# A windowed attention with a gated output layer: the last output block in two column halves, two blocks gathered in the scores' banks, and another written-out order

## Chip, cores and metric

The kernel runs on one core of one Trainium2 chip. The metric is device time in microseconds (us) of one launch. A core has TensorE (PE in the profile, with its weight loads as PEld), VectorE (DVE), ScalarE (ACT), GpSimd (POOL) and SyncE (SP). Here SP issues nearly all DMA transfers; ACT issues three at the start.

## What is computed

```python
# q, k, v: (4, 8, 768, 64) float32; w_val, w_out: (512, 512) float64; conv_w: (5, 512) float64
scores = q @ k.T / 8                       # kept where key < 4 (sinks) or 0 <= row - key < 128
a = softmax(scores, over kept keys);  x = a @ v           # heads joined: (4, 768, 512)
gate = sigmoid(causal 5-tap convolution of x along the rows, per column, weights conv_w)
out = ((gate * (x @ w_val)) @ w_out)       # (4, 768, 512) float32
```

## The kernel before

**Tiling.** The 768 rows of each of 4 batches are cut into 3 parts of 256 rows; with two quads of heads that makes 24 steps `s` (batch, part, quad). Two steps make one block `m` of 256 rows and all 512 columns, so there are 12 blocks. Each block gives two output blocks of 128 rows, `i` = 0 and 1.

**Stages of a step.** `kq`, `vv` load queries, keys and values (three buffers each). `s0`, `s1` are the score matmuls of two head pairs (line 391, on parts of 64x32 of the TensorE array), masked and reduced to a maximum on DVE; `e0`, `e1` are the exponentials on ACT; `rec` and `norm` normalise (ACT, DVE, POOL); `tx` transposes the weights on TensorE (line 449, whole array), `px` and `py` copy them out of PSUM; `sk`, `ts` do the same for the four sink keys (line 454, whole array); `vl` multiplies with the values (line 504, parts of 64x64) and `si` adds the sinks (line 511, whole array). `xc`, `xh`, `hd`, `xl`, `c4`, `c0`, `c1`, `th` take the result out of PSUM, split it into a high and a low part for exact products, and form the gate.

**Stages of a block.** `v0` to `v3` are the products with `w_val` (line 566), `v0`, `v1` the halves of one 512-column bank and `v2`, `v3` of the next; `g0`, `g1` gate them (DVE), `h0`, `h1`, `l0`, `l1` split again (ACT, POOL). `o0` and `o1` are the two halves of the contraction with `w_out` for output block 0 (`outp`, line 606), `o2` and `o3` those for block 1, and `t0`, `t1` copy the result out of PSUM with factor 0.5 (`store`, line 610) and store it (line 613). The weights come as float64 and are taken apart on the chip in stages `wv?` and `wo?` (`wvl` loads, `wva` to `wvf` decode).

**PSUM.** Of eight banks of 512 columns, four form two pairs `pr` that `scores` and `probs_t` take in turn through `pair()`, two hold `xv`, and two, `homes`, serve `val`, `outp`, the sinks' transposes and the weights' decoding: each takes one off the list and gives it back.

**Order.** The string `ORDER` names every stage once. Inside `tc.manual_schedule()` it is walked from left to right, and every engine runs its own instructions in that order (SP's DMA issues too); semaphores set the rest. `fill.n` are n TensorE matmuls on zeros. `flag`, computed on DVE, decides between this path and a general one (`tc.If`, line 781): each engine loads it into a register (line 780) and branches. Those loads stand outside the written-out order; the scheduler places them.

Of the kernel before, what the change touches and what calls it, by code (L numbers as in the profile page):

```python
# [36 lines left out]
blanks wvl.0 load_conv kq.0 masks signs leads fill.5 wvl.1 conv_weights wvl.2 wva.0 wvb.0 s0.0 kq.1 wvd.0
wvc.0 s1.0 wve.0 fill.4 wva.1 wvb.1 e0.0 wva.2 e1.0 wvb.2 wvc.2 fill.7 wvd.1 wol.0 kq.2 s1.1 wvc.1 rec.0 wvl.3
s0.1 fill.10 s1.2 wvf.0 woa.0 e1.1 wve.1 e0.1 wob.0 norm.0 tx.0 px.0 e1.2 woc.0 rec.1 py.0 vv.0 fill.6 sv.0
sk.0 ts.0 wod.0 wva.3 norm.1 s0.2 e0.2 vl.0 kq.8 kq.3 s0.3 wvf.1 si.0 xc.0 woe.0 wvb.3 xh.0 tx.1 c4.0 rec.2  # L40
wof.0 wol.2 wol.1 wvc.3 fill.6 hd.0 wvd.2 wve.2 px.1 wvd.3 kq.4 wve.3 e0.3 c0.0 c1.0 woa.1 wob.1 wvf.2 norm.2
vv.3 py.1 vv.1 sv.1 xl.0 tx.2 py.2 sk.1 px.2 woc.1 ts.1 vl.1 s1.3 wvf.3 wod.1 si.1 xc.1 c4.1 sk.2 ts.2 s0.4
hd.1 xh.1 xl.1 c0.1 woe.1 e1.3 wol.3 rec.3 woa.3 c1.1 wob.3 e0.4 v0.0 v1.0 th.0 y0.0 norm.3 vv.2 g0.0 vl.2
woa.2 wob.2 h0.0 l0.0 th.1 s1.4 kq.6 kq.5 wof.1 woe.3 e1.4 v2.0 v3.0 y1.0 tx.3 py.3 si.2 xc.2 woe.2 hd.2 xh.2
g1.0 px.3 wof.2 wod.2 s0.6 c4.2 c0.2 h1.0 o0.0 l1.0 o2.0 e0.6 wof.3 s0.5 c1.2 rec.4 xl.2 s1.6 wod.3 o1.0 o3.0
t0.0 norm.4 sk.3 e0.5 ts.3 t1.0 vl.3 si.3 xh.3 xc.3 xl.3 s1.5 e1.6 tx.4 px.4 vv.5 sk.4 ts.4 hd.3 c4.3 c0.3
e1.5 rec.5 norm.5 v0.1 v1.1 y0.1 py.4 c1.3 th.2 v2.1 v3.1 g0.1 h0.1 kq.7 s0.7 vv.4 th.3 vl.4 y1.1 g1.1 vv.6
l0.1 s1.7 rec.6 sv.6 s1.8 h1.1 si.4 xh.4 l1.1 xc.4 hd.4 e0.7 o2.1 o3.1 c4.4 c0.4 xl.4 e1.8 kq.10 kq.9 c1.4
norm.6 tx.5 o0.1 t1.1 py.5 o1.1 px.5 sk.5 e1.7 tx.6 rec.7 px.6 ts.5 t0.1 py.6 vl.5 si.5 xc.5 hd.5 xh.5 s0.9
e0.9 sk.6 ts.6 s0.8 e0.8 c4.5 c0.5 c1.5 xl.5 vv.7 v0.2 rec.8 v1.2 norm.7 tx.7 py.7 px.7 th.4 g0.2 v2.2 s1.9  # L50
s1.10 norm.8 th.5 h0.2 e1.9 vl.6 si.6 sk.7 vv.8 v3.2 ts.7 xc.6 hd.6 xh.6 l0.2 g1.2 rec.9 o0.2 c4.6 h1.2 l1.2
o2.2 o3.2 sv.7 e1.10 c0.6 kq.11 tx.8 c1.6 py.8 vl.7 px.8 norm.9 s0.10 si.7 t1.2 sk.8 xl.6 xc.7 hd.7 xh.7 ts.8
kq.12 c4.7 tx.9 px.9 c0.7 c1.7 e0.10 rec.10 py.9 xl.7 th.6 o1.2 norm.10 v0.3 v1.3 vv.10 g0.3 h0.3 s0.12 s0.11
t0.2 vl.8 si.8 s1.11 e0.12 xc.8 hd.8 c4.8 sk.9 ts.9 l0.3 kq.13 th.7 vv.9 xh.8 e0.11 e1.11 c0.8 c1.8 v2.3 v3.3
o2.3 xl.8 g1.3 s1.12 s1.13 vl.9 si.9 h1.3 tx.10 l1.3 o3.3 e1.12 rec.12 rec.11 px.10 xc.9 hd.9 xh.9 py.10 c4.9
c0.9 t1.3 o0.3 o1.3 c1.9 th.9 t0.3 sk.10 ts.10 xl.9 vv.11 norm.11 s0.13 vl.10 si.10 xc.10 c4.10 hd.10 xh.10
norm.12 kq.15 tx.11 px.11 py.11 th.8 e0.13 v0.4 v1.4 v2.4 v3.4 c0.10 c1.10 g0.4 sk.11 ts.11 e1.13 g1.4 h0.4
l0.4 kq.14 tx.12 py.12 vl.11 px.12 s0.14 s1.14 rec.13 si.11 h1.4 sk.12 ts.12 o0.4 l1.4 o1.4 vv.12 o2.4 o3.4
sv.12 xc.11 c4.11 hd.11 xh.11 c0.11 vv.13 c1.11 e0.14 sv.13 kq.18 s0.18 norm.13 e1.14 rec.14 kq.16 s0.15 xl.10
t1.4 vl.12 si.12 th.11 xc.12 hd.12 xh.12 xl.11 c4.12 t0.4 xl.12 tx.13 norm.14 px.13 v2.5 v3.5 c0.12 g1.5 py.13  # L60
th.10 c1.12 e0.15 v0.5 v1.5 g0.5 sk.13 ts.13 h0.5 l0.5 vv.14 s1.15 e1.15 s1.18 rec.15 kq.19 vl.13 si.13 xc.13
hd.13 xh.13 o0.5 s0.16 h1.5 kq.17 tx.14 px.14 c4.13 c0.13 c1.13 l1.5 o2.5 o3.5 th.12 e0.16 o1.5 norm.15 t1.5
py.14 warm_up tx.15 py.15 t0.5 sk.14 ts.14 s1.16 vl.14 si.14 vv.17 e1.18 xc.14 hd.14 xh.14 sk.15 ts.15 xl.13
px.15 e1.16 c4.14 vv.15 v2.6 v0.6 v1.6 c0.14 c1.14 rec.16 g0.6 s0.17 xl.14 e0.18 h0.6 e0.17 s0.19 rec.18 vl.15
norm.16 v3.6 l0.6 th.13 si.15 vv.16 g1.6 s1.19 xc.15 th.14 c4.15 hd.15 xh.15 s1.17 sk.16 o0.6 ts.16 kq.20 h1.6
l1.6 xl.15 tx.16 o1.6 v0.7 v1.7 e0.19 px.16 c0.15 e1.17 rec.17 t0.6 kq.21 c1.15 s0.20 py.16 vl.16 si.16
norm.18 vv.21 sk.18 ts.18 vv.18 e1.19 xc.16 hd.16 g0.7 norm.17 rec.19 e0.20 tx.18 px.18 py.18 c4.16 c0.16
th.15 xh.16 v2.7 v3.7 xl.16 h0.7 g1.7 tx.17 h1.7 px.17 l1.7 c1.16 py.17 o2.6 o3.6 s1.20 s0.21 t1.6 vl.17 sk.17
ts.17 l0.7 o0.7 si.17 e1.20 xc.17 hd.17 xh.17 norm.19 tx.19 c4.17 vv.19 c0.17 sv.18 c1.17 xl.17 o1.7 kq.22
o2.7 o3.7 py.19 e0.21 rec.20 norm.20 px.19 t1.7 s1.21 scalars vl.18 t0.7 si.18 xc.18 hd.18 xh.18 c4.18 c0.18  # L70
sv.19 th.17 tx.20 px.20 e1.21 vv.22 rec.21 th.16 v2.8 v3.8 v0.8 v1.8 g1.8 h1.8 c1.18 g0.8 sk.19 ts.19 py.20
h0.8 s1.22 kq.23 s0.22 vl.19 si.19 xc.19 hd.19 xh.19 xl.18 l1.8 sk.20 l0.8 vv.20 o0.8 ts.20 c4.19 c0.19 c1.19
norm.21 e1.22 e0.22 rec.22 o1.8 o2.8 tx.21 py.21 px.21 t0.8 vl.20 xl.19 s1.23 s0.23 si.20 xc.20 norm.22 hd.20
xh.20 e1.23 th.18 v0.9 v1.9 g0.9 c4.20 c0.20 e0.23 rec.23 o3.8 t1.8 tx.22 v2.9 v3.9 h0.9 py.22 c1.20 sk.21
l0.9 norm.23 th.20 ts.21 th.19 vl.21 si.21 g1.9 px.22 xc.21 hd.21 xh.21 tx.23 px.23 o0.9 o2.9 c4.21 c0.21
c1.21 h1.9 l1.9 xl.20 o3.9 t1.9 o1.9 py.23 sk.22 ts.22 t0.9 vl.22 xl.21 si.22 xc.22 sk.23 v0.10 v1.10 xh.22
# [113 lines left out]
def banded(ctx, tc, wts, cw, zero, ident, warm_up, scalars, flag, qt, kt, vt, vsk, w_val, conv_w, w_out, out):  # L190
# [406 lines left out]
    def outp(m, i, h):  # L597
        wh, wl = wts["wo"]
        gh, gl = gs[m]
        if h == 0:  # L600
            vacc[m, 2 + i] = homes.pop(0)
        acc = vacc[m, 2 + i]
        ts = slice(i * P, (i + 1) * P)
        for kc in (0, 1) if h == 0 else (2, 3):
            for n, (a, x) in enumerate(((gh, wh), (gh, wl), (gl, wh))):
                nc.tensor.matmul(acc, a[:, kc, ts], x[:, kc], start=(kc + n == 0), stop=(kc + n == 5))  # L606

    def store(m, i):
        ob = p2.tile([P, DM], F32, name="osb", tag="osb", bufs=3)
        nc.scalar.activation(out=ob, in_=vacc[m, 2 + i], func=AF.Copy, scale=0.5)  # L610
# [2 lines left out]
        nc.sync.dma_start(out=out[m // NP, at:at + P, :], in_=ob)

# [232 lines left out]
```

## Time and profile before

| | |
|---|---|
| median of 3 runs (lowest, highest) | 271.04 us (270.05, 272.22) |
| profiled execution: its time, its span | 270.55 us, 268.7 us |
| TensorE busy | 258.3 us (96%), 3760 matmuls |
| DVE, ACT, POOL busy | 205.4, 189.1, 176.2 us |
| DMA | 36.93 MB, mean 137 GB/s |
| last output copy starts, ends | 261.75, 262.35 us |

The span is the time between the first and the last event that the profile holds; the execution lies 1.85 us above it. Rows of the chain of waits and of the timeline give the start in us from the span's start, the length in us, the engine, the output tile (or output and input) and the line; a count x n stands behind merged rows. Groups of instructions give busy time and the mean ns of one. Matmuls overlap in the records, so a TensorE row of the chain (start to next start) is the better measure of what a matmul costs than its own length.

### The profile page before, as it was taken

The numbers are of one execution on the slowest core, as the hardware profiler recorded it, in microseconds if no ns is written. First come the engines' busy times: TensorE is split into PE (matmuls) and PEld (weight loads), VectorE is DVE, ScalarE is ACT, GpSimd is POOL, SyncE is SP. The second block draws the span as 40 slices with busy tenths as digits, with TensorE's granted clock in tenths as the row PEclk, the third lists the DMA queues.
The fourth block names the chain that finished last, engine by engine and source line by source line (L and its number), as shares of the span: only waits on it lengthen the run. The fifth ranks groups of instructions, "written<-read, shape, count | busy, mean of one in ns | idle before, by whom it ended". The sixth has DMA issues, their size and how long they took to land.

```text
span 268.7 us, 9474 instructions
## 1 busy us (share of the span) xinstructions
PE 258.3 (96%) x3760; PEld 213.6 (79%) x3760; DVE 205.4 (76%) x561; ACT 189.1 (70%) x667; POOL 176.2 (66%) x233
## 2 busy tenths in 40 slices
PE   7899999999999999999999999999999999999990
...
DMA packets 27394, 36.93 MB, mean 137 GB/s; under 512 B 2256, under 2 KB 23760, under 8 KB 27344
## 3 DMA queue, kind: packets, MB, share of 16 engines
...
q14 instruction: 19, 0.16, 0.2%
...
## 4 chain that ended last, share of the span: by engine, by line
PE 83%; ACT 9%; POOL 2%; DMA 2%; issue 1%; DVE 0%; POOLq 0%; ACTq 0%
PE ac L606 25%; PE ac L566 25%; PE xv L504 11%; PE pr L391 10%; PE pr L449 7%; ACT w L416 4%; PE xv L511 3%; DMA raw<-in_w_val_dram 2%; PE ac L454 1%; POOL xl L534 1%; ACT wvh L151 1%; ACT wv_p L137 1%; ACT wv_p L156 1%; ACT wvl L183 1%; POOL wo_f L157 0%
## 5 line engine op out<-in xcount | busy, mean ns | idle before, releaser
L547 DVE SCALAR_TENSOR_TENSOR sg<-xv,cw,sg 128x256 f32<-128x256 f32 x192 | 77.8, 474 | 12.4 <-POOL sg L539 7.0
L431 POOL TENSOR_TENSOR wx<-w,sm 128x512 f32<-128x512 f32 x48 | 49.1, 1044 | 11.3 <-DVE sm L423 11.1
L416 ACT ACTIVATE w<-pr,ngm 128x132 f32<-128x132 f32 x136 | 48.5, 369 | 1.7
L595 POOL TENSOR_TENSOR gl<-sg,gh 128x512 fp32r<-128x512 f32 x24 | 31.0, 1295 | 28.1 <-ACT gh L591 28.0
L566 PE MATMUL ac<-xh,wvh 128*128 128x256 f32 x192 | 48.4, 286 | 0.0
L566 PE MATMUL ac<-xh,wvl 128*128 128x256 f32 x192 | 47.1, 279 | 0.0
L606 PE MATMUL ac<-woh,gh 128*128 128x512 f32 x96 | 39.2, 408 | 0.0
L539 POOL TENSOR_TENSOR sg<-xt,cw 128x512 f32<-128x512 f32 x24 | 25.0, 1043 | 20.6 <-ACT xt L518 20.6
L606 PE MATMUL ac<-wol,gh 128*128 128x512 f32 x96 | 38.0, 396 | 0.0
L606 PE MATMUL ac<-woh,gl 128*128 128x512 f32 x96 | 38.0, 395 | 0.0
L566 PEld LDWEIGHTS ac<-xh,wvh 128*128 128x128 f32 x192 | 36.1, 188 | 0.8 <-issue 0.5
L566 PEld LDWEIGHTS ac<-xh,wvl 128*128 128x128 f32 x192 | 36.2, 188 | 0.2
L391 PE MATMUL pr<-k,q 64*32 64x168 f32 x1536 | 35.3, 307 | 0.7 <-DMA q<-in_qt_dram 0.6
L504 PEld LDWEIGHTS xv<-wt,v 64*64 64x64 f32 x1024 | 30.4, 133 | 7.0 <-issue 4.5
L504 PE MATMUL xv<-wt,v 64*64 64x192 f32 (+2 forms) x1024 | 34.5, 278 | 0.2 <-PE ac L566 0.2
L534 POOL TENSOR_TENSOR xl<-xt,xh 128x512 fp32r<-128x512 f32 x24 | 30.8, 1289 | 3.2 <-ACT xh L526 2.8
L566 PE MATMUL ac<-xl,wvh 128*128 128x256 f32 x192 | 30.7, 280 | 0.4 <-POOL xl L534 0.4
L391 PEld LDWEIGHTS pr<-k,q 64*32 64x32 f32 x1536 | 23.8, 106 | 7.9 <-issue 2.6
L396 DVE COPY_PREDICATED pr<-low,pr 128x256 f32<-128x256 uint8 x48 | 20.3, 423 | 12.2 <-PE pr L391 12.2
L591 ACT ACTIVATE gh<-sg 128x512 fp32r<-128x512 f32 x24 | 15.0, 628 | 19.2 <-DVE sg L585 19.2
L416 ACT ACTIVATION_READ_ACCUMULATOR w<-pr,ngm 128x1 f32 x136 | 27.6, 203 | 0.0
L518 ACT ACTIVATE xt<-xv 128x512 f32<-128x512 f32 x24 | 14.4, 600 | 17.3 <-PE xv L511 17.2
...
## 6 DMA issues: line engine op xcount, KB each, us to landing
...
out_dram<-osb SPq DMA_DIRECT2D x24, 256.0 KB, 2.2
q<-in_qt_dram SPq DMA_DIRECT2D x23, 256.0 KB, 5.4
...
v<-in_vt_dram SPq DMA_DIRECT2D x8, 256.0 KB, 5.2
...
```

The source lines that it names most:

```text
L391: nc.tensor.matmul(ss[e * QB:(e + 1) * QB, j, c * n + x0:c * n + x1], q[js, g, (4 * c + e) * QB:(4 * c + e + 1) * QB], k[js, g, (2 * c + e ...
L396: nc.vector.copy_predicated(sv[:, :, :, :D], low[:, None, None, :].to_broadcast([P, 2, 2, D]), sv[:, :, :, 2 * HB:])
L416: nc.scalar.activation(out=w[:, g, j, c], in_=sx[:, j, c, :PK], func=AF.Exp, scale=0.125 if whole else -1.0, bias=ngm[:, g, j, c:c + 1], a ...
L431: nc.gpsimd.tensor_tensor(out=t[:, n].rearrange("p c h x -> p h c x"), in0=w[:, :, :, at], in1=sm.to_broadcast([P, 4, 2, D]), op=ALU.mult)
L449: nc.tensor.transpose(out=x[:, n, o:o + P], identity=ident, in_=ws[s][:, n, c, 2 * g:2 * g + 2].rearrange("p j x -> p (j x)"))
L504: nc.tensor.matmul(acc[o * D:(o + 1) * D, g, x0 + h * D:x0 + (h + a1 - a0 + 1) * D], v[js, g, n], t[js, g, n, a0:a1 + 1].rearrange("p a r ...
L534: nc.gpsimd.tensor_tensor(out=half(xls, s, "xl", F32R), in0=xts[s], in1=half(xhs, s, "xh", F32R).bitcast(F32), op=ALU.subtract)
L539: nc.gpsimd.tensor_tensor(out=half(sg, s, "sg", F32), in0=xts[s], op=ALU.mult, in1=cw[:, g, KT - 1:].to_broadcast([P, 2, PQ]))
L547: nc.vector.scalar_tensor_tensor(out=g, in0=x, scalar=a, in1=g, op0=ALU.mult, op1=ALU.add)
L566: nc.tensor.matmul(acc[:, h], a[:, kc, cs], x[:, kc], start=(n == 0), stop=(n == 11))
L595: nc.gpsimd.tensor_tensor(out=gl, in0=g, in1=gh.bitcast(F32), op=ALU.subtract)
L606: nc.tensor.matmul(acc, a[:, kc, ts], x[:, kc], start=(kc + n == 0), stop=(kc + n == 5))
```

## The change

Three things change. Output block (`m` 11, `i` 1), the last, is computed by columns: `o2.11` now makes columns 0 to 255 over the whole contraction (12 matmuls of 256 columns), `o3.11` columns 256 to 511, which go to a bank of `homes`; each half has its own copy of 128x256 and its own store of 128 KB (`piece`). Blocks 10 and 11 (`MP` is 10) gather their output in a pair of the scores' banks instead of `homes`. And the whole `ORDER` is another one, with the same 825 names.

```diff
+MP = 10
+LAST = (B * NP - 1, 1)
...
     def outp(m, i, h):
         wh, wl = wts["wo"]
         gh, gl = gs[m]
-        if h == 0:
+        if m >= MP:
+            if m not in outs:
+                outs[m] = pair()
+            vacc[m, 2 + i] = outs[m][:, i]
+        elif h == 0:
             vacc[m, 2 + i] = homes.pop(0)
         acc = vacc[m, 2 + i]
         ts = slice(i * P, (i + 1) * P)
+        if (m, i) == LAST:
+            if h:
+                piece(m, i, 0)
+                vacc[m, 2 + i] = acc = homes.pop(0)
+            cs = slice(h * PQ, (h + 1) * PQ)
+            for kc in range(4):
+                for n, (a, x) in enumerate(((gh, wh), (gh, wl), (gl, wh))):
+                    nc.tensor.matmul(acc[:, cs], a[:, kc, ts], x[:, kc, cs], start=(kc + n == 0), stop=(kc + n == 5))
+            return
...
+    def piece(m, i, h):
+        if h == 0:
+            obs[m, i] = p2.tile([P, DM], F32, name="osb", tag="osb", bufs=3)
+        cs = slice(h * PQ, (h + 1) * PQ)
+        nc.scalar.activation(out=obs[m, i][:, cs], in_=vacc[m, 2 + i][:, cs], func=AF.Copy, scale=0.5)
+        at = (2 * (m % NP) + i) * P
+        nc.sync.dma_start(out=out[m // NP, at:at + P, cs], in_=obs[m, i][:, cs])
+
     def store(m, i):
+        if (m, i) == LAST:
+            piece(m, i, 1)
+            homes.append(vacc[m, 2 + i])
+            return
         ob = p2.tile([P, DM], F32, name="osb", tag="osb", bufs=3)
         nc.scalar.activation(out=ob, in_=vacc[m, 2 + i], func=AF.Copy, scale=0.5)
-        homes.append(vacc[m, 2 + i])
+        if m < MP:
+            homes.append(vacc[m, 2 + i])
```

Of the two orders, the first stages, three places in the middle and the end (`-` before, `+` after):

```
- blanks wvl.0 load_conv kq.0 masks signs leads fill.5 wvl.1 conv_weights wvl.2 wva.0 wvb.0 s0.0 kq.1 wvd.0 wvc.0 s1.0 wve.0
+ wvl.0 masks load_conv fill.5 kq.0 signs leads conv_weights wva.0 wvb.0 wvc.0 s0.0 s1.0 wvd.0 wve.0 wvl.1 wva.1
+ s1.11 xc.8 hd.8 rec.10 c4.8 xh.8 e0.11 xl.8 th.7 kq.13 sk.9 ts.9 c0.8 c1.8 norm.10 e1.11 v2.3 v3.3 g1.3 o2.3 s1.12 e0.12 s1.13
+ s0.10 py.8 sk.8 ts.8 si.7 ... tx.9 px.9 o1.2 ... v0.3 v1.3 ... kq.12 g0.3 s0.12 kq.11 s0.11
+ o3.5 c0.13 norm.15 t1.5 c1.13 px.14 sk.14 tx.15 ts.14 s1.16 py.15 vl.14 si.14 e0.18 xc.14 hd.14 sk.15 xh.14 kq.19 px.15 e1.16
+   ts.15 xl.13 v0.6 v1.6 v2.6 th.13 c4.14 c0.14 c1.14 g0.6 rec.16 xl.14 e1.18 kq.17 vv.15 norm.16 kq.21 s0.17 s0.19
- h1.10 l1.10 xl.22 o0.10 o1.10 c4.23 c0.23 xl.23 t0.10 c1.23 o3.10 v0.11 th.22 v1.11 t1.10 v2.11 v3.11 g0.11 th.23 g1.11 h0.11
-   l0.11 o2.11 h1.11 l1.11 o0.11 o1.11 flag t0.11 o3.11 t1.11
+ o0.10 xl.23 o2.10 v0.11 v1.11 g1.10 c0.23 v2.11 h1.10 l1.10 v3.11 c1.23 th.22 g0.11 th.23 h0.11 g1.11 o1.10
+   h1.11 l0.11 o0.11 l1.11 t0.10 o1.11 o3.10 t0.11 o2.11 t1.10 o3.11 t1.11 warm_up flag
```

Ahead of `v0.0` the two orders hold the same stages of ACT, DVE, POOL and TensorE, in other places; `blanks` moves behind `s1.1`, `scalars` from step 21 to step 9, `warm_up` (one ACT instruction) from step 14 to the end. The order of the `kq` loads is 0 1 2 8 3 4 6 5 7 10 9 11 12 13 15 14 18 16 19 17 20 21 22 23 before, and 0 1 2 3 7 4 5 6 10 8 9 18 12 11 13 14 15 16 19 17 21 20 22 23 after. TensorE's own order from `v0.0` on, with S for `s0` or `s1`, V for `vl` (both on parts of the array), i for `si`, x for `tx`, k for `sk`, F for a `v` or `o` stage (whole array):

```
before FFVSFFxiSFFSSFFkViSxkFFFFSVSSiFFxFFkxViSkSFFxFSSVikFFFFxVSikxFFFSSViSkFFFSSVixFFFkSVixFFFFkxVSSikFFFFSSVixFFFFkSSV
       iFSxFFFxkSVikFFFSSVFiSSkFxFFFSVikxFFxFFSSVkFixFFFSVixFFFFkSSVikFFFxVSSiFFFxFFkVixFFFFkVikFFFFFViFFFFFFFFFFF
after  FFSVFFxiFSFSSFFkViSxkFFFFSVSSiFFxFFkxViSkSFFxFSSVikFFFFxVSkixFFFSSViSkFFFSSVixFFFxkSVixFFFFkSSVikFFFFSSVixFFFFkSSV
       iFSxFFFkxSVikFFFSSViFSSkFFxFFSVixFkxFFFkSSVFixFFFSVixFFFFkVikSSFFFxViSSFFxFFFkVixFFFFkVikFFFFViFFFFFFFFFFFF
```

More of the change, by code (lines that the diff above doesn't have):

```diff
@@ L36 @@
 ORDER = """
[L37 to L76, printed above, removed]
@@ L77 @@
-ts.23 v2.10 v3.10 g0.10 c4.22 hd.22 c0.22 c1.22 th.21 g1.10 h0.10 l0.10 o2.10 vv.23 vl.23 h1.10 si.23 xc.23
-hd.23 xh.23 l1.10 xl.22 o0.10 o1.10 c4.23 c0.23 xl.23 t0.10 c1.23 o3.10 v0.11 th.22 v1.11 t1.10 v2.11 v3.11
-g0.11 th.23 g1.11 h0.11 l0.11 o2.11 h1.11 l1.11 o0.11 o1.11 flag t0.11 o3.11 t1.11
+wvl.0 masks load_conv fill.5 kq.0 signs leads conv_weights wva.0 wvb.0 wvc.0 s0.0 s1.0 wvd.0 wve.0 wvl.1 wva.1
+e0.0 wvl.2 wva.2 fill.7 wvb.1 kq.1 e1.0 wvb.2 wvc.2 fill.4 rec.0 wvc.1 wol.0 wvf.0 wvd.1 woa.0 kq.2 s1.1
@@ new lines @@
+blanks e1.1 s0.1 e0.1 fill.10 s1.2 wve.1 e1.2 wvl.3 wob.0 norm.0 woc.0 tx.0 px.0 fill.6 kq.3 rec.1 py.0 vv.0
+sv.0 kq.7 sk.0 ts.0 vv.2 wod.0 wva.3 s0.2 e0.2 s0.3 vl.0 kq.4 wvf.1 si.0 xh.0 woe.0 wvb.3 xc.0 wol.1 rec.2
+norm.1 tx.1 px.1 c4.0 wvc.3 fill.6 hd.0 wvd.2 c0.0 c1.0 vv.6 wve.2 wof.0 wvd.3 wve.3 e0.3 woa.1 wob.1 norm.2
+py.1 vv.1 sv.1 wvf.3 wvf.2 tx.2 py.2 px.2 wol.3 s1.3 sk.1 vl.1 xl.0 sk.2 ts.1 si.1 woc.1 wod.1 xc.1 c4.1 s0.4
+ts.2 hd.1 xh.1 c0.1 xl.1 e1.3 rec.3 woa.3 c1.1 e0.4 wob.3 woe.1 v0.0 norm.3 v1.0 th.0 y0.0 g0.0 wol.2 woa.2
@@ new lines @@
+wob.2 s1.4 vl.2 h0.0 l0.0 woe.3 wof.1 th.1 v2.0 v3.0 vv.4 e1.4 tx.3 woe.2 wof.2 si.2 y1.0 g1.0 kq.5 px.3 wod.3
+xc.2 hd.2 xh.2 o2.0 wod.2 c4.2 h1.0 l1.0 py.3 kq.6 s0.6 e0.6 o0.0 c0.2 s0.5 wof.3 c1.2 rec.4 s1.6 vv.3 o1.0
+t0.0 e0.5 o3.0 sk.3 ts.3 t1.0 vl.3 si.3 xh.3 s1.5 xl.2 norm.4 xc.3 hd.3 tx.4 xl.3 px.4 sk.4 kq.10 ts.4 c4.3
+e1.5 rec.5 norm.5 e1.6 py.4 c0.3 v0.1 v1.1 y0.1 c1.3 th.2 g0.1 v2.1 v3.1 rec.6 h0.1 y1.1 s0.7 th.3 g1.1 l0.1
+vl.4 s1.7 kq.8 s1.8 h1.1 l1.1 si.4 o2.1 o3.1 xc.4 xh.4 hd.4 c4.4 c0.4 e0.7 xl.4 e1.8 norm.6 kq.9 sv.6 vv.5
@@ new lines @@
+tx.5 px.5 o0.1 o1.1 c1.4 t1.1 py.5 e1.7 rec.7 sk.5 ts.5 tx.6 py.6 t0.1 vl.5 si.5 xc.5 c4.5 px.6 hd.5 xh.5 th.4
+s0.9 sk.6 ts.6 s0.8 e0.9 xl.5 v0.2 v1.2 c0.5 c1.5 norm.7 tx.7 e0.8 rec.8 norm.8 py.7 px.7 g0.2 v2.2 s1.9 h0.2
+scalars s1.10 l0.2 vv.7 kq.18 th.5 vl.6 si.6 sv.7 xc.6 c4.6 hd.6 xh.6 sk.7 v3.2 ts.7 g1.2 h1.2 c0.6 e1.9 o0.2
+l1.2 o2.2 e1.10 c1.6 rec.9 o3.2 t1.2 tx.8 xl.6 px.8 vl.7 s0.10 py.8 sk.8 ts.8 si.7 xc.7 hd.7 norm.9 c4.7 xh.7
+tx.9 px.9 o1.2 e0.10 xl.7 v0.3 v1.3 c0.7 c1.7 th.6 py.9 kq.12 g0.3 s0.12 kq.11 s0.11 vv.8 h0.3 vl.8 si.8 l0.3
@@ new lines @@
+t0.2 vv.12 s1.11 xc.8 hd.8 rec.10 c4.8 xh.8 e0.11 xl.8 th.7 kq.13 sk.9 ts.9 c0.8 c1.8 norm.10 e1.11 v2.3 v3.3
+g1.3 o2.3 s1.12 e0.12 s1.13 vv.9 vl.9 si.9 h1.3 e1.12 rec.11 l1.3 rec.12 tx.10 o3.3 px.10 xc.9 hd.9 c4.9 o0.3
+norm.11 xh.9 vv.10 py.10 t1.3 xl.9 c0.9 c1.9 e1.13 o1.3 t0.3 tx.11 py.11 sk.10 ts.10 px.11 vl.10 s0.13 si.10
+xc.10 hd.10 norm.12 vv.11 tx.12 px.12 v0.4 v1.4 xh.10 v2.4 th.8 v3.4 vv.13 c4.10 c0.10 g0.4 h0.4 c1.10 l0.4
+kq.14 py.12 sv.12 th.9 g1.4 kq.15 sk.11 ts.11 s1.14 h1.4 s0.14 xl.10 e1.14 kq.16 vl.11 si.11 xc.11 hd.11 sk.12
@@ new lines @@
+ts.12 xh.11 e0.13 l1.4 o0.4 o1.4 o2.4 o3.4 c4.11 c0.11 c1.11 rec.13 e0.14 rec.14 s0.18 t1.4 s0.15 t0.4 vv.18
+xl.11 vl.12 si.12 norm.13 xc.12 hd.12 c4.12 tx.13 sv.13 th.11 xh.12 px.13 c0.12 py.13 e0.15 th.10 xl.12
+norm.14 c1.12 v0.5 v2.5 v3.5 g1.5 v1.5 g0.5 h0.5 h1.5 l0.5 sk.13 ts.13 s1.15 vv.14 s1.18 l1.5 vl.13 e1.15
+si.13 xc.13 hd.13 th.12 rec.15 o0.5 s0.16 xh.13 tx.14 py.14 c4.13 e0.16 o1.5 t0.5 o2.5 o3.5 c0.13 norm.15 t1.5
+c1.13 px.14 sk.14 tx.15 ts.14 s1.16 py.15 vl.14 si.14 e0.18 xc.14 hd.14 sk.15 xh.14 kq.19 px.15 e1.16 ts.15
```

15 lines of the change are left out of this document (added).

## The prediction

> **What bounds the kernel now.** I read the page's busy shares and slices first, then the chain of waits in order of time, then the instructions on each queue at the end, to find where TensorE is not already full.
>
> ```profile
> PE 258.3 (96%) x3760; PEld 213.6 (79%) x3760; DVE 205.4 (76%) x561; ACT 189.1 (70%) x667; POOL 176.2 (66%) x233
> PE   7899999999999999999999999999999999999990
> ```
>
> TensorE is full in all slices but the first two and the last. The chain in order of time shows where it takes over:
>
> ```profile
> 37.53 1.26 POOL xl L534
> 38.84 1.92 PE ac L566 x14
> ...
> 242.97 1.40 PE ac L606 x6
> 244.37 1.48 PE xv L504 x48
> ...
> 250.47 5.61 PE ac L566 x48
> 256.08 5.60 PE ac L606 x24
> 261.75 0.60 ACT osb L610
> ```
>
> So there are three stretches. Up to 38.84 us the chain runs over the first weight load, ACT and, last, POOL, and TensorE has matmuls on zeros between its work. From 38.84 to 261.68 (256.08 plus 5.60), 222.8 us, it is TensorE alone. Then come a copy and 6.35 us to the end of the span at 268.7. The change takes no work from TensorE, so a gain can lie only in the first stretch, in the third, and in the seams of the second.
>
> **The head.** The timeline of ACT and DVE, where ACT starts on the first weights:
>
> ```profile
> 5.80 0.66 ACT L137 ACTIVATE wv_p<-raw 128x512 f32<-128x512 f32 x1
> 7.71 0.63 ACT L151 ACTIVATE wvh<-wv_t 128x512 fp32r<-128x512 f32 x1 [1.25 <-DVE wv_t L142]
> 8.25 0.66 ACT L156 ACTIVATE wv_p<-raw 128x512 f32<-128x512 uint32 x1
> 8.51 0.71 DVE L400 TENSOR_REDUCE ngm<-pr 128x4 f32<-128x528 f32 x1
> 9.45 0.19 ACT L413 ACTIVATE ngm<-ngm 128x4 f32<-128x4 f32 x1
> ```
>
> ACT waits 1.25 us for DVE. The new order puts `wvc.0` (8.25, 0.6 us) ahead of `wvd.0` (7.71), into that wait. But `e0.0`, the next stage but one, needs the maximum that DVE has at 8.51 + 0.71 = 9.22, and it starts at 9.45 now: at most 0.2 us comes through. From there ACT and POOL have the same stages up to `v0.0`, which `xl.1` on POOL (37.53 to 38.79) releases. The six memsets' worth of `blanks` lie in POOL's early slack in both. I take 0.15 us off. The bounds are 0.5 off and 0.5 on, since the loads of steps 3 and 7 now pass others on a full queue; `wol.1`, behind `kq.4`, is then the next that could be late.
>
> **The seams.** A whole-array stage costs more behind a stage on parts of the array:
>
> ```profile
> 161.25 0.44 PE xv L511 x2
> 161.69 0.11 PE ac L454
> 161.80 4.21 PE ac L566 x36
> 166.00 1.30 PE pr L391 x64
> 167.30 1.48 PE xv L504 x48
> 168.78 1.59 PE ac L566 x12
> 170.37 0.23 PE xv L511 x2
> 170.61 1.30 PE pr L391 x64
> 171.91 0.26 PE ac L454
> 172.17 1.41 PE ac L606 x6
> 173.57 0.87 PE pr L449 x8
> ```
>
> Behind scores `sk` (line 454) takes 0.26, behind `si` 0.11; a `v` stage takes 1.59 behind `vl`, where a third of 4.21 is 1.40; `si` (line 511) takes 0.44 behind `vl` and 0.23 behind a `v`. That is 0.15 to 0.21 us for each change from parts to the whole. In the two lines of letters I count an S or V followed by i, x, k or F 30 times before and 32 times after: two more at 0.17, 0.35 us on. Unbroken runs of S number 26 in both, so what a change between the other kinds may cost stays as it is.
>
> The Trainium skill ("TensorEngine Tiling (Array Packing)", Tiling Modes, Key Properties) says that changing the tiling mode drains TensorE. By that, S beside V (64x32 beside 64x64) would pay too; of these neighbours the new order has 16 where the old has 18, and this term would be zero. The trace does not show that: `vl` takes 1.48 behind scores (167.30) and behind an `o` stage (244.37).
>
> **The loads.** SP issues loads in order, behind stores and behind waits for a free buffer.
>
> ```profile
> L238 SPq DMA_DIRECT2D q<-in_qt_dram x23: 368/462/1839, 6.2 to 202.1; - x23
> DMA to landing us min/median/max: 3.6/5.4/8.8
> ```
>
> The keys are issued first, which takes about as long as the queries' 0.46 at most, say 0.4. From a free buffer to landed queries that makes 0.4 + 5.4 = 5.8 us in the median, 4.0 at best, 9.2 at worst. `kq.18`, loaded at step 7, holds one of three buffers until `s1.18`, so steps 10 to 17 share two. `kq.13` then gets the buffer of step 11, free after `s1.11`; up to `s1.13` TensorE has `sk.9`, `v2.3`, `v3.3`, `o2.3`, `s1.12`, by the rows above 0.26 + 3 x 1.40 + 0.65 = 5.1 us. That is 0.7 short in the median. Behind its wait on SP stands `vv.9`, which `vl.9` needs 0.6 us later than `s1.13`. `kq.11` (buffer of step 10, free after `s0.10`) has `sk`, `si`, `tx`, `o1`, two `v` and `s0.12`: 0.26 + 0.23 + 0.87 + 3 x 1.40 + 0.65 = 6.2, just enough. `kq.17` stands behind `t1.5` and `kq.19`: a copy of 0.6, four issues, 1.7 with gaps, and 5.4 to land make 7.7; TensorE has `sk`, `tx`, `s1`, `vl`, `si`, `sk` and three `v`, 7.9. A late load stops TensorE and all behind it. I take 0.5 us for the three, between nothing (queue empty) and the median's 0.7; bounds 0 and 2.5.
>
> **The tail.** The instructions behind the last store, by line:
>
> ```profile
> L780 SPq TENSOR_LOAD <-flag_i x1: 477/477/477, 259.1 to 259.1; - x1
> L780 SPq SEQ_ASSERT  x1: 33/33/33, 259.9 to 259.9; - x1
> L781 SPq EVENT_SEMAPHORE  x8: 17/17/17, 266.8 to 267.3; - x8
> L781 DVEq COMPARE_BRANCH  x1: 72/72/72, 259.8 to 259.8; - x1
> L781 ACTq COMPARE_BRANCH  x1: 54/54/54, 262.6 to 262.6; - x1
> L781 SPq COMPARE_BRANCH  x1: 45/45/45, 262.8 to 262.8; - x1
> L781 DVEq EVENT_SEMAPHORE  x1: 21/21/21, 262.8 to 262.8; - x1
> L781 ACTq EVENT_SEMAPHORE  x1: 17/17/17, 263.0 to 263.0; - x1
> L613 SPq DMA_DIRECT2D out_dram<-osb x24: 332/357/376, 54.8 to 262.4; - x24
> out_dram<-osb SPq DMA_DIRECT2D x1, 256.0 KB, 3.1
> L530 ACT ACTIVATE xv<-xt 128x8 f32<-128x8 f32 x16 | 2.9, 181 | 0.4
> ```
>
> SP issues the last store at 262.4 and branches at 262.8; its next instruction runs at 266.8, 4.0 us later, and 1.9 us are left. The store lands 3.1 us after its issue, at 265.5, hidden by 1.3 us. So the column halves help only as far as SP issues sooner. A copy of 256 columns isn't in the trace; between 0.18 us (8 columns) and 0.60 (512) I interpolate 0.39: 0.2 us off, bounds 0 and 0.4. TensorE takes 5.61 us for 48 matmuls of 256 columns and 5.60 for 24 of 512, so `o2.11` and `o3.11` stay at 1.40 each. The first half's copy and store lie beside `o3.11`; without that cover they would cost about 0.4 each. The scores' banks are free by then, `tx.23` being long past, and TensorE has no gap from 250.47 on that `homes` could have made: zero, where a wait for a bank would cost a copy, 0.6. `warm_up` comes on ACT behind its last copy; ACT is past its branch at 263.0, 3.8 us ahead of SP, which covers its 0.2.
>
> SP's 4.0 us behind the branch are longer than DVE's 3.0 (259.8 to 262.8), before the last two stores. If their traffic makes the difference, half the bytes could give back up to half of it; I take 0.3 off, bounds 0 and 1.0.
>
> **The sum.** 0.15 off, 0.35 on, 0.5 on, 0.2 off, 0.3 off: 0.2 us on. Against the profiled execution's 270.55 that is 270.75; the median of the runs shown, 271.04, lies 0.5 above that execution, so the forecast is 271.2.
>
> **Rivals.** *A, slower: loads come late.* If queries land 1 us over the median at `kq.11`, `kq.13` and `kq.17`, TensorE waits 0.6 + 1.7 + 0.8 = 3.1 us for my 0.5: 273.8. It decides from queries landing about 6 us after issue on. For it: landings go up to 8.8, and two buffers do the work of three. Against: little else is in the queue at these places, and 3.6 is seen. A mild form, 1.5 to 2.5 us in all, gives 272.2 to 273.2.
>
> *B, faster: SP's 4.0 us go.* ACT needs 0.4 us for its branch (262.6 to 263.0), so the wait isn't owed by every engine. Without it the last store's landing bounds, 265.5 less 0.2 for the copy, and with the 1.9 us behind it the span ends at 267.2, 1.5 off; with the head, seams and loads (0.7 on) that is 270.2, and with these at their good bounds 269.2. Against: nothing in the diff touches the branch. The Trainium skill ("Runtime: NRT & Kernel Launch", Instruction fetch mechanics) says that a taken branch waits for a fetch unless its target lies in the two pages at hand; that the engines here wait 0.4, 3.0 and 4.0 us agrees with it, and no row tells where the pages lie.
>
> *C, the tail doesn't do what it says.* `flag` now stands last; if SP's register load and its arithmetic (259.1 to 259.9) go behind the last store instead of ahead of it, 0.8 us come on: 272.0. Against: DVE runs `flag` behind `g1.11` in both.
>
> **How the numbers follow.** Forecast, 270.2 to 272.0: 0.64. A: 0.18, of it 0.07 over 273.75. B: 0.10, of it 0.03 under 268.33 (head and seams better than their bounds). C: 0.08. A measurement of this kernel tells about 1% (2.7 us) from no change: faster 0.03, within 0.90, slower 0.07. The range takes the forecast, C, A's mild form and most of B, 269.4 to 273.2, and leaves out about 0.15.
>
> **What would show it.** Right: `v0.0` released by `xl.1` within 0.5 us of 38.8; TensorE's stretch from there 0.3 to 1 us longer, with waits for `in_qt_dram` ahead of `s1.13`; a last copy near 0.39 us; SP's branch 0.4 us behind it and 3.5 to 4 us of nothing. Wrong: TensorE waiting on another engine (a fault that the order's distances did not show me), an SP gap far from 4 us, a head that moves by more than 0.5 us, or seams that cost nothing.

## The result: 272.86 us, 0.6% slower than before

| | before | after |
|---|---|---|
| median, runs side by side | 271.23 us (22) | 272.86 us (22) |
| ratio to before, 95% interval | | 1.0061 (1.0042 to 1.008) |
| profiled execution: time, span | 270.55, 268.7 us | 272.91, 270.9 us |
| TensorE takes over, ends | 38.84, 261.68 us | 38.65, 265.53 us |
| from TensorE's end to the end of the span | 7.0 us | 5.4 us |

The forecast was 271.2 us, with a range of 269.4 to 273.2 and "within 1%" as the likeliest. The median lies in the range, 1.7 us over the forecast, and the change within 1%. TensorE's stretch grew by 4.0 us (226.9 for 222.8), the tail shrank by 1.6, the head by 0.2: +2.2, the difference of the spans. This execution lies at the median of its kernel, that of before 0.7 under its own.

### The profile after

The instruction of TensorE that `xl.1` on POOL releases, from the timeline:

```profile
38.65 0.50 PE L568 MATMUL ac<-xl,wvh 128*128 128x256 f32 x2 [0.42 <-POOL xl L536]
```

The busy shares on the page, with TensorE at 96% as before:

```profile
PE 259.4 (96%) x3768; PEld 214.6 (79%) x3772; DVE 204.8 (76%) x561; ACT 188.7 (70%) x668; POOL 176.1 (65%) x233
```

So the share doesn't show it. The table by stage does; it gives, for each stretch of time, its length, the busy time of PE, PEld, DVE, ACT and POOL with instructions, the granted clock, the DMA engines' busy share and GB/s. The changed kernel:

```profile
95.00:104.80 9.80, 8.15 (x145) 7.08 (x147) 8.92 (x26) 5.97 (x18) 5.80 (x8) 1.00 0.64 207
104.80:116.00 11.20, 10.78 (x257) 8.92 (x257) 8.38 (x28) 8.16 (x37) 6.44 (x9) 1.00 0.61 193
...
165.00:172.00 7.00, 5.93 (x134) 5.46 (x136) 5.47 (x15) 5.63 (x24) 4.14 (x5) 1.00 0.98 331
```

and the same stretches before:

```profile
95.00:104.80 9.80, 9.80 (x203) 8.72 (x206) 9.01 (x27) 6.56 (x20) 6.72 (x9) 1.00 0.43 140
104.80:116.00 11.20, 11.20 (x214) 9.62 (x205) 10.21 (x38) 10.18 (x44) 6.69 (x9) 1.00 0.38 122
165.00:172.00 7.00, 7.00 (x201) 6.10 (x199) 5.93 (x22) 5.65 (x24) 4.55 (x7) 1.00 0.40 143
```

All of the new idle time lies in three short stretches (between 116 and 165 us TensorE is busy for 49.00 us of 49.00, from 172 to 262 for 90.00 of 90.00): 1.65, 0.42 and 1.07 us, 3.14 together. They are the places of `kq.11`, `kq.13` and `kq.17`, at a full clock. The last column but one says more: the DMA engines were 64%, 61% and 98% busy there, before 43%, 38% and 40%. (With 0.35 for the seams that makes 3.5 of the 4.0 us. The rest is in the waits too: matmuls overlap in the records, so a pause from start to start is longer than the idle time. `s0.12` and `s0.11` took 3.33 us together, from 102.28 to 104.73 plus 0.88; unhindered they take 1.30, by a row shown below, which is 2.0 more for 1.65 idle.) What TensorE waited for, by the page's reckoning:

```profile
PE pr L393 <- DMA q<-in_qt_dram: 1.6, 1, 1.6
...
PE pr L393 <- ACT w L418: 1.1, 1, 1.1
```

The first is a load, the second is put down to ACT's exponentials. The chain that ended in the first wait, in order of time:

```profile
93.76 0.91 ACT w L418 x5
...
94.77 0.49 ACT osb L640
...
95.28 0.36 SPq L644
...
96.15 0.66 SPq L238
...
96.87 0.54 SPq L240
...
97.51 0.41 SPq L238
...
97.98 6.62 DMA q<-in_qt_dram
...
104.73 0.88 PE pr L393 x32
```

Read it from below: `s0.11` starts at 104.73, its queries were issued at 97.98 and took 6.62 us. Ahead of them on SP stand the keys, then the load of step 12 (96.15, 96.87), then the store `t1.2`, which waited for a copy on ACT that had stood behind exponentials. For the second wait I read SP's queue in the timeline:

```profile
159.12 2.38 SPq L644 DMA_DIRECT2D out_dram<-osb  x2
161.59 0.79 SPq L238 DMA_DIRECT2D k<-in_kt_dram  x1
162.43 0.47 SPq L240 DMA_DIRECT2D q<-in_qt_dram  x1
163.00 0.42 SPq L238 DMA_DIRECT2D k<-in_kt_dram  x1
163.47 0.46 SPq L240 DMA_DIRECT2D q<-in_qt_dram  x1
```

and, in the view of the line of code, the landing of the three query loads issued between 162 and 166 us:

```profile
DMA to landing us min/median/max: 3.7/5.9/7.3
```

The three are `kq.19`, `kq.17` and `kq.21` in this order, and each took longer than the one ahead of it. (An estimate of why: keys and queries of a step are 408 and 256 KB, which take about 2 us to move at the 331 GB/s of the stretch from 165 us on; SP issued the second pair 1.0 us behind the first, and the third, with values between, 1.5 us behind the second.) `kq.17`, the middle one, landed at 163.47 + 5.9 = 169.4; `s0.17` started at 169.50. ACT's last exponential ended at 169.41, so the page named ACT.

The tail: the last matmuls and the last copy in the chain.

```profile
264.10 1.43 PE ac L617 x12
...
265.55 0.38 ACT osb L630
```

The instructions on SP's queue, by line of code:

```profile
L811 SPq TENSOR_LOAD <-flag_i x1: 532/532/532, 260.2 to 260.2; - x1
L812 SPq EVENT_SEMAPHORE  x8: 17/17/17, 269.0 to 269.5; - x8
L812 SPq COMPARE_BRANCH  x1: 45/45/45, 266.3 to 266.3; - x1
L632 SPq DMA_DIRECT2D out_dram<-osb x2: 332/332/333, 264.6 to 266.0; - x2
```

SP issues the last store at 266.0, branches at 266.3 and goes on at 269.0: 2.7 us of nothing instead of 4.0.

### The profile page after: what moved, and what is told of

It reads as the page before. It is cut to its first block, busy times and chain, and to the rows that moved or that the text cites. A ratio compares the mean times of both kernels' runs of the same rounds, so it can differ in the third digit from the quotient of the medians.

```text
span 270.9 us, 9515 instructions
## 1 busy us (share of the span) xinstructions
PE 259.4 (96%) x3768; PEld 214.6 (79%) x3772; DVE 204.8 (76%) x561; ACT 188.7 (70%) x668; POOL 176.1 (65%) x233
## 4 chain that ended last, share of the span: by engine, by line
PE 73%; ACT 10%; POOL 5%; DVE 5%; DMA 2%; issue 2%; SPq 1%; POOLq 0%; ACTq 0%; DVEq 0%
PE ac L568 19%; PE ac L621 17%; PE xv L506 10%; PE pr L393 9%; PE pr L451 6%; ACT w L418 5%; PE xv L513 3%; PE pr L621 3%; DMA q<-in_qt_dram 2%; DVE sg L549 2%; POOL wx L433 1%; PE ac L456 1%; PE ac L226 1%; POOL sg L541 1%; DVE sg L587 1%
## 5 line engine op out<-in xcount | busy, mean ns | idle before, releaser
L621 PE MATMUL ac<-woh,gh 128*128 128x512 f32 x80 | 32.9, 411 | 0.0
L621 PE MATMUL ac<-wol,gh 128*128 128x512 f32 x80 | 31.7, 396 | 0.0
L621 PE MATMUL ac<-woh,gl 128*128 128x512 f32 x80 | 31.6, 395 | 0.0
```

## The experiments

My theory after this: the order loses 3 to 3.6 us because queries come late at three places (the load behind another load on SP), and the tail gives 1.6 back, 0.2 by the smaller copy and the rest by SP's shorter gap. Rivals: ACT holds the scores' banks at `s0.17`; the seams; the gap goes with the order and not with the store.

### The loads of steps 17 and 19 earlier

```diff
-... o0.5 s0.16 ... xh.14 kq.19 px.15 ... e1.18 kq.17 vv.15 ...
+... o0.5 kq.17 kq.19 s0.16 ... xh.14 px.15 ... e1.18 vv.15 ...
```

> The changed kernel with the loads of steps 17 and 19 issued ahead of s0.16, some 8 us earlier, and nothing else moved. Theory (s0.17 waits for its queries, which landed at 169.36 us, 0.14 ahead of it): no wait of TensorE at s0.17, 1.1 us less. Rival (the scores' banks are held by the exponentials of step 18 on ACT, as the profile's waits name it, whose last record ends at 169.40): s0.17 still waits about 1.1 us.

One execution. TensorE in the stretch where the changed kernel lost 1.07 us:

```profile
165.00:172.00 7.00, 7.00 (x144) 6.51 (x137) 6.06 (x15) 6.20 (x26) 2.85 (x3) 1.00 0.57 199
```

No idle time at all, and no wait for ACT at `s0.17` among the waits. So it was the load, and the page's "ACT" was the neighbour that ended last. (The total of this execution, 273.73 us, can't be used: the granted clock was 0.67 and 0.50 between 106 and 110 us.)

### The load of step 12 as well

```diff
-... o3.2 t1.2 ... py.9 kq.12 g0.3 s0.12 kq.11 s0.11
+... o3.2 kq.12 t1.2 ... py.9 g0.3 s0.12 kq.11 s0.11
```

(with the edit above)

> The same, and the load of step 12 ahead of the copy and store t1.2 instead of 16 stages behind it, so that the load of step 11 behind it on SP can go as soon as its buffer is free. Theory (s0.11 waits because both loads stand behind the store, whose copy is late on ACT): the wait at s0.11 falls from 2.0 us to under 0.4, with the 1.1 us of step 17 about 2.7 to 3.1 us less than the changed kernel, 269.8 to 270.2 us, ratio to before 0.995; TensorE's stretch from v0.0 then exceeds that of before by 0.4 to 0.9 us, the two added seams and the rest. Rival (the buffer of step 10 sets the load of step 11): its issue moves by less than 0.3 us, the wait stays near 2 us, and only 1.1 us is won.

271.99 us, ratio 1.0034 (1.0016 to 1.0052): 0.9 us under the changed kernel, where I expected 2.7 to 3.1. The keys of step 11 now went out at 96.94, 0.6 us earlier, and the queries landed 3.7 us after issue for 6.62: no wait at `s0.11`. But the chain shows a new one:

```profile
102.42 1.30 PE pr L393 x64
...
106.93 6.25 DMA q<-in_qt_dram
...
113.31 0.88 PE pr L393 x32
```

The first row is `s0.12` and `s0.11` without a pause, the last `s1.13`: 1.8 us of waiting, where the changed kernel had a quarter of one. TensorE came 2 us sooner, and the queries, issued 2 us sooner too, took 6.25 us for 4.4. The wait had moved to the next load that two buffers squeezed.

### Every load one place ahead

```diff
-vv.7 kq.18 th.5 ... o3.2 t1.2 ... py.9 kq.12 g0.3 s0.12 kq.11 s0.11 ... kq.13 sk.9 ... kq.14 py.12 ... kq.15 sk.11
+vv.7 kq.12 th.5 ... o3.2 kq.11 t1.2 ... py.9 kq.13 g0.3 s0.12 s0.11 ... kq.14 sk.9 ... kq.15 py.12 ... kq.18 sk.11
```

(with the first edit)

> The changed kernel, but step 18 no longer loads at step 7: each load of steps 12, 11, 13, 14, 15 takes the place of the one ahead of it (so three buffers serve steps 10 to 17), step 18 loads where step 15 did, and steps 17 and 19 load ahead of s0.16. All else as it is. Theory (step 18's early load makes two buffers do the work of three, so that the wait only moved from s0.11 to s1.13 when one load was moved): no wait of TensorE for queries after v0.0, TensorE's end at 261.9 us within 0.4 (before's 261.7, 0.2 off at the head, 0.35 on for two seams), the tail 5.3 us, 268.9 to 269.6 us, ratio to before 0.993. Rival 1 (landings vary and something else of the order costs about 2 us): TensorE's end at 263 or later though no wait for queries is left. Rival 2 (the transport of 680 KB a step is the limit, not the buffers): a wait of 1 us or more appears at another load.

271.17 us, ratio 1.0015 (0.9996 to 1.0034). No wait for queries is left between 95 and 172 us, but TensorE ended at 263.3, not at 261.9: that is what rival 1 had named as its sign. What stood behind it is nearer to rival 2, another load, though 0.8 us and not 1 or more, at `vl.9` (and `v0.0` came 0.1 later than before, not 0.2 sooner). The wait:

```profile
PE xv L506 <- DVE ngm L407: 0.8, 1, 0.8
```

In the timeline the loads that brought the values of step 9 and, behind them, of another step, and the landing of the first of the two by its line of code:

```profile
107.68 1.81 SPq L247 DMA_DIRECT2D v<-in_vt_dram  x2
```

```profile
DMA to landing us min/median/max: 5.4/5.4/5.4
```

The page again names the neighbour: values issued at 107.68 landed at 113.1, and `vl.9` started at 113.20. In this order `vv.9` stands behind `kq.14`, which waits for its buffer.

### Step 9's values ahead of step 14's queries, and the last store on ACT

```diff
-... kq.14 sk.9 ... s1.13 vv.9 vl.9
+... vv.9 kq.14 sk.9 ... s1.13 vl.9
```

(with the edit above and that of the store on ACT, below)

> The kernel with the loads one ahead and the last store on ACT (ratio 0.9949), with the values of step 9 loaded ahead of the queries of step 14 instead of behind them. Theory (the wait at vl.9, 0.9 us, which the profile puts down to DVE, is for these values, which landed 0.13 us ahead of it): no wait at vl.9, TensorE's stretch from v0.0 within 0.8 us of before's 224.8, ratio 0.992. Rival (DVE holds vl.9 by its masking of s1.13): the wait at vl.9 stays 0.8 to 0.9 us and the ratio 0.995.

268.81 us, ratio 0.993 (0.9906 to 0.9954), against 0.9949 (0.993 to 0.9968) without this edit. These intervals overlap; the trace of the one profiled execution is clearer, with no wait at `vl.9`.

```profile
95.00:104.80 9.80, 9.80 (x179) 8.67 (x178) 8.66 (x20) 6.29 (x25) 5.41 (x8) 1.00 0.42 139
104.80:116.00 11.20, 11.20 (x251) 9.57 (x236) 10.12 (x42) 9.97 (x44) 7.61 (x9) 1.00 0.61 194
165.00:172.00 7.00, 7.00 (x160) 6.37 (x165) 6.08 (x22) 6.32 (x29) 3.89 (x7) 1.00 0.24 84
```

The three stretches are as full as before. From the first `v0.0` matmul to TensorE's end this execution took 224.88 us (38.69 to 263.57), before 224.54 (37.14 to 261.68): the 0.34 left over is what two more seams were priced at. (The shift of the waits inside is as large, so this agrees with the price and doesn't prove it.) So the loss of the order was loads, and nothing else of its size.

### The order of before with the new end

```diff
 ... (order of before, to xl.22 of step 22) ...
-o0.10 o1.10 c4.23 ... o3.10 v0.11 ... v3.11 g0.11 ... o2.11 h1.11 l1.11 o0.11 o1.11 flag t0.11 o3.11 t1.11
+o0.10 c4.23 c0.23 xl.23 c1.23 v0.11 ... v3.11 h0.11 g1.11 o1.10 ... o1.11 o3.10 t0.11 o2.11 t1.10 o3.11 t1.11 flag
```

> The order of the kernel before up to step 23's last stages, and behind them the last two blocks as the change has them: output of blocks 10 and 11 in the scores' banks, last block in two column halves, its stages in a row that the halves allow. Theory (the loss sits in the order, the gain in the tail): TensorE's stretch keeps the length of before, 222.8 us within 0.3, and the tail is the changed kernel's 5.4 us for 7.0: about 1.6 us faster than before, ratio 0.994. Rival 1 (the short gap of SP belongs to the other order, not to the smaller last store): the gap behind SP's branch is 4.0 us again, and only the copy's 0.2 us is won, ratio 0.999. Rival 2 (the banks or the halves cost TensorE something at the end): TensorE's end comes 0.5 us or more later than 261.7.

271.68 us, ratio 1.0021 (1.0005 to 1.0037) for the expected 0.994: missed, and rival 2's sign, a later end of TensorE, came. The tail was 5.2 us as in the changed kernel, with a gap of 2.5 us, so the gap does not need the new order. But TensorE ended at 263.71: of the 2.0 us, 1.4 were a wait for `xl.23` on POOL, since my end had taken `o1.10` and `o3.10`, which had filled that time, from ahead of `v0.11`. That was a fault of my end. Taken to the letter from the change:

```diff
-... sk.23 v0.10 v1.10 xh.22 ts.23 v2.10 ...          (before, from here on)
+... sk.23 v0.10 v1.10 xh.22 ts.23 v2.10 v3.10 ... xc.23 xl.22 ... o0.10 xl.23 o2.10 v0.11 v1.11 g1.10 ... t1.11 flag
```

> The order of the kernel before up to the copy of step 23's sinks, and from there the changed kernel's order to the letter (without its late warm-up), with the banks and the column halves. In the run with an end of my own TensorE lost 1.4 us to x_low of step 23 on POOL, which here stands where the change has it. Theory (the end is worth what the tail shows): no such wait, TensorE's end within 0.3 of 261.7, tail 5.3 us for 7.0, 269.3 us, ratio 0.994. Rival (the end's order costs TensorE as much as the tail gains): TensorE's end at 263 or later and the ratio within 0.002 of 1.

269.74 us, ratio 0.9962 (0.9934 to 0.999), for the expected 0.994. TensorE's end 262.23, 0.5 us later than before, tail 5.5 us. The change's end by itself is worth about 1.0 us on the old order, by the interval 0.3 to 1.8.

### The new order with a whole last store, and the banks alone

```diff
-LAST = (B * NP - 1, 1)
+LAST = None
```

> The changed kernel, order and banks as they are, but the last output block again by halves of the contraction, with one copy and one store of 256 KB. Theory (the bytes of the last store lengthen SP's gap): last copy 0.60 us, gap behind the branch about 4.0 us for 2.6, so about 1.6 us slower than the changed kernel, 274.5 us, ratio to before 1.012. Rival 1 (the gap goes with the order): gap 2.6 us, 0.2 us slower than the changed kernel, 273.1 us, ratio 1.007.

274.0 us, ratio 1.01 (1.0079 to 1.0121): 0.4% over the changed kernel. Last copy 0.60 us, and SP:

```profile
L812 SPq EVENT_SEMAPHORE  x8: 17/17/17, 269.9 to 270.4; - x8
...
L812 SPq COMPARE_BRANCH  x1: 45/45/45, 266.5 to 266.5; - x1
```

3.4 us, longer than the changed kernel's 2.7, shorter than before's 4.0 and the 4.0 expected. The tail is 6.4 us. Then the changed code under the order of before, with the same one-line edit, so that only the banks are new:

> The kernel before, order and whole last store included, with blocks 10 and 11 gathered in the scores' banks and nothing else changed. Theory (the banks are worth nothing by themselves, they only permit the other end): ratio 1.000 within 0.002, TensorE's end within 0.3 us of 261.7, gap behind SP's branch 3.4 to 4.0 us. Rival (the banks take waits off TensorE at the end): TensorE's end 0.5 us or more earlier.

271.49 us, ratio 1.0043 (1.0016 to 1.007): slower, where the theory said the same and the rival faster, and the chain says why.

```profile
247.73 2.82 PE pr L621 x12
...
250.57 0.61 ACT osb L640
...
251.22 1.66 PE pr L621 x6
252.88 5.60 PE ac L568 x48
258.48 4.20 PE pr L621 x18
...
262.70 0.61 ACT osb L640
...
263.35 1.67 PE pr L621 x6
```

`o3.10` writes the other bank of the pair that `t0.10` is copying, and waits until the copy is done; `o3.11` likewise. Twice 0.67 us. In the order of before `t0` stands right ahead of `o3`; in the new one `o1.11`, 1.4 us, lies between. So the banks cost by themselves; in the new end, with that stage between, no such wait shows. (The same execution stood still for 1.32 us inside `s1.8` with its clock at 1.00 and nothing named; this stays unexplained.)

### What makes SP's gap

The change without its last store of 128 KB, and without both stores of the last block:

```diff
     def piece(m, i, h):
...
-        nc.sync.dma_start(out=out[m // NP, at:at + P, cs], in_=obs[m, i][:, cs])
+        if h == 0:
+            nc.sync.dma_start(out=out[m // NP, at:at + P, cs], in_=obs[m, i][:, cs])
```

> The changed kernel without the store of the last 256 columns of the last block; the copy stays. The output lacks that piece. Theory (SP's gap behind its branch grows with the bytes that it has just sent, 4.0 and 3.4 us with 256 KB, 2.5 to 2.8 with 128 KB in flight): SP branches behind the first half's store, some 1.4 us earlier, and its gap is again about 2.6 us or less, over before TensorE has been done 2.5 us. Rival (the gap is one fetch of code, whatever flies): the gap is 2.6 us, and what is left at the end is ACT's copy and the other engines' branches.

> The changed kernel without both stores of the last block; the copies stay, and the output lacks the block. The last store that SP issues is then 256 KB, of the block before. Theory (256 KB in flight make SP's gap longer): gap behind SP's branch 3.4 to 4.0 us, as in the two kernels whose last store is whole. Rival (the gap follows SP's code, which has two instructions less here, or has a floor of 2.5 us that whole stores only happened to exceed): 2.5 to 2.8 us.

One execution each. Without the last store the gap is 2.5 us (265.2 to 267.7), the store in flight being the first half's, and the tail 3.9 us. Theory and rival both allow that, so this run doesn't decide between them. Without both

```profile
L812 SPq EVENT_SEMAPHORE  x8: 17/17/17, 269.9 to 270.4; - x8
L812 SPq COMPARE_BRANCH  x1: 45/45/45, 266.8 to 266.8; - x1
```

3.1 us, between what theory and rival had said. And the store moved to ACT, in the kernel with the loads one ahead:

```diff
-        nc.sync.dma_start(out=out[m // NP, at:at + P, cs], in_=obs[m, i][:, cs])
+        (nc.scalar if h else nc.sync).dma_start(out=out[m // NP, at:at + P, cs], in_=obs[m, i][:, cs])
```

> The kernel with the loads one ahead, and the store of the last half issued by ACT, right behind its copy, instead of by SP. SP then branches behind the first half's store. Theory (SP's gap behind its branch starts with the branch and is not owed to the last store's landing): SP's gap is over about 1 us earlier, the end is then set by ACT's issue and the store's landing (1.7 us after issue in the changed kernel), 0.5 to 1.0 us faster than the kernel with the loads one ahead. Rival (ACT pays SP's gap in SP's place, as it now branches last): no gain within 0.3 us, the gap of 2.6 us shows behind ACT's branch.

269.59 us, ratio 0.9949 (0.993 to 0.9968), for 1.0015 with SP's store: 1.6 us, more than the 0.5 to 1.0 expected.

```profile
L812 SPq EVENT_SEMAPHORE  x8: 17/17/17, 265.2 to 265.7; - x8
...
L812 SPq COMPARE_BRANCH  x1: 45/45/45, 262.6 to 262.6; - x1
L812 ACTq COMPARE_BRANCH  x1: 62/62/62, 264.7 to 264.7; - x1
L812 ACTq EVENT_SEMAPHORE  x1: 17/17/17, 265.2 to 265.2; - x1
```

SP branches 0.6 us ahead of the last copy (263.2), and its 2.6 us run beside that copy and the store; ACT, now last, pays 0.5. The tail falls to 3.9 us. (Little more can be won there: TensorE has a branch too, 3.5 to 4.1 us in the rows of its weight loads in all fourteen kernels, and here it goes on at 265.5, no sooner than SP and ACT.) All SP gaps by what SP had last sent:

| last store of SP | SP's gap, us |
|---|---|
| 256 KB | 4.0 before, 3.4 whole store, 2.9 banks alone, 3.1 no store of the last block |
| 128 KB | 2.7 after, 2.5 and 2.5 new end, 2.8 and 2.7 other loads, 2.7 steps 17 and 19 earlier, 2.5 without last store, 2.6, 2.6 and 2.7 store on ACT |

Four values of 2.9 to 4.0 beside ten of 2.5 to 2.8, with orders and instruction counts mixed in both rows and one execution for each: the longer gaps go with the larger store, 0.4 to 1.5 us over a floor near 2.5. That the bytes in flight are the cause is likely and not shown, as two gaps with the same 256 KB differ by 1.1. The floor isn't made by a store of the engine's own: DVE, which stores nothing, stands still for 2.8 to 3.2 us behind its branch in all fourteen kernels. The DMA view shows packets of instructions in SP's gap, here in the kernel before, from 262.4 to 264.9 us (queue, kind, packets, MB, share of the 16 engines):

```profile
q14 instruction: 3, 0.02, 3.3%
q8 instruction: 1, 0.02, 2.3%
```

In all fourteen executions such packets of 8 KB start within 1.4 us of SP's branch. In the ten with 128 KB SP goes on 1.0 to 1.3 us after the last of them has ended, in the other four 1.3 to 2.3 us. A fetch of code would fit; but the rows don't say which engine the packets are for, so what SP waits for stays open. That ACT gets by with 0.5 agrees with the Trainium skill ("Runtime: NRT & Kernel Launch", Instruction fetch mechanics), by which a taken branch waits only where its target isn't at hand; no run shows where the targets lay.

### A version that beats both

The order of before with the change's end, and the last store on ACT.

> The order of before with the changed kernel's end (ratio 0.9962 to before by itself), and the store of the last half issued by ACT. Theory (ACT's issue takes SP's gap off the end, and the two gains are independent): TensorE's end as before within 0.5 us of 261.7, tail 4.0 us instead of 5.4 (measured with the loads one ahead), 268.3 us, ratio 0.990. Rival (the loads-one-ahead kernel won its 1.6 us at TensorE, not in the tail): tail 5.3 us, ratio 0.996.

268.14 us, ratio 0.9913 (0.9885 to 0.9941). TensorE's end 262.22, tail 4.2 us: the two gains add up, and the forecast of 268.3 held. The new order with all its loads in time and the same end gave 0.993, and the intervals overlap: a gain by the order itself isn't shown.

## Why the prediction was right, and where it wasn't

The range held and the sum missed by 1.7 us, because two mis-sized terms partly cancelled: the loads were priced 2.6 to 3.2 us too low, and the tail's gain 1.1 too low. That the time fell into the range is in part luck: with the loads at their measured price and the tail as forecast it would have been 273.8 or more, outside the range.

- **Head, 0.15 off.** Here 0.19 off (38.65 for 38.84), within the bound of 0.5. But over the runs `v0.0`'s first matmul came at 36.9 to 38.7 us with the new head (nine executions, median 37.2) and at 36.8 to 37.2 with the old (five, median 37.1): the term is no gain, rather 0.2 on.
- **Seams, 0.35 on.** The run with all loads in time leaves 0.34. The other working, to zero, doesn't come out of its rule. By the Trainium skill ("TensorEngine Tiling (Array Packing)", Tiling Modes, Key Properties) every change of the tiling mode drains TensorE, so the changes from the whole array to parts count too, and they had been left out: of all changes the letters of the two orders hold 78 before and 80 after, two more again, of the same sign as the 0.34, and no run here tells the two prices apart. The row of `vl`, 1.48 us behind scores and behind an `o` stage, couldn't decide either, as the mode changes at both places. (For `vl.10` and `s0.13` the letters of the order after stand the wrong way round, S V for V S; the counts are the same.)
- **Loads, 0.5 on: the step that failed.** The three places, the two buffers and the wait on SP were as the prediction named them; the price was 3.1 us idle, above the term's bound of 2.5, and what rival A had worked out for queries 1 us over the median. A's point of decision, a landing about 6 us after issue, held too: 6.6 and 5.9. Mis-sized were both halves of "0.4 + 5.4 = 5.8". From the free buffer to the queries' issue it wasn't 0.4: `s0.10` left the buffer of step 10 at 96.72, where the next stage on TensorE starts, and the queries went at 97.98, 1.3 us, because SP was still issuing the load of step 12 behind a store that ACT had delayed. And 5.4 is no price for a landing: it is a median over loads that go alone and loads that follow another. In the two rows looked at, the first landed in 3.7 us both times, the second in 5.9 and 6.6, the third in 7.3. `kq.11` and `kq.17` were seconds, so 1.3 + 6.6 = 7.9 us stood against the 6.2 that TensorE had (the prediction's own figure); for `kq.17` 8.9 stood for 7.7 against 7.9 (queries at 163.47, 3.0 behind the end of `o3.5` instead of 2.3, and 5.9). `kq.13`, named as the one most short, landed in 4.4 and cost only a quarter of a us; when TensorE came sooner, it cost 1.8.
- **Copy, 0.2 off.** 0.38 us for the interpolated 0.39, and SP's branch 0.4 us behind it, as named.
- **SP's gap, 0.3 off, bounds 0 and 1.0.** 1.3 off in these two executions, outside the bounds. The direction (half the bytes, a shorter gap) agrees with all runs. But before's 4.0 was the longest of its kind, so a part of the 1.3 belongs to that one execution. Nor was DVE's 3.0, with which the prediction compared it, clear of the stores: one was issued at 260.93, inside it. The change's end measured by itself gave 1.0 us with the copy included.
- **Banks, zero.** Right here, as an order had put a stage between copy and next matmul; the 0.6 named as the price of a wait for a bank came twice, 0.67 each, once that cover was gone.
- **Rivals.** A's mechanism took place, and beside it the tail gave 1.6 us, as much as B had worked out (1.5), though SP's wait of 2.7 us remained; that is why the total lay between forecast and A. C did not: SP loaded its register at 260.2, ahead of the last stores, though `flag` stood last. (B's 269.2 doesn't follow from the bounds given: head 0.5 off, loads 0 and seams 0.35 make 269.4.)
- **Signs.** Of those named for being right, the last copy and SP's branch came. TensorE's stretch grew by 4.0 us and not by 0.3 to 1, SP's gap was 2.7 us and not 3.5 to 4, and the waits stood ahead of `s0.11` and `s0.17` and not of `s1.13`. Of those named for being wrong, "TensorE waiting on another engine" appeared in the page's list, and was a load all the same.
